# A transformer block on one core: a new instruction order, first-MLP partial sums split by token group, and a zero fill moved to the DMA queue

## The chip, the cores and the metric

The kernel runs on one core of a Trainium2 chip. A core has a matrix engine (PE, with its weight loads listed as PEld), a vector engine (DVE), a scalar engine (ACT), a general engine (POOL, also called GpSimd) and a sync engine (SP) which in this kernel issues nearly all the DMAs. Every engine works through its own list of instructions in order and waits on semaphores for the others. The metric is the device time of one execution in microseconds; the kernel before the change has a median of 255.73 us over three runs (255.32 to 256.43).

## The reference

One block on 2048 tokens of 512 features. A conditioning vector gives six modulation vectors (shift, scale and gate for each half). The first half is a layer norm, a modulation, and attention with 32 heads of 16 features in which a token sees itself and the 255 tokens before it. The second half is a layer norm, a modulation, another layer norm, and an MLP that mixes *tokens*: it contracts over the 2048 tokens, not over the features.

```python
h = _layernorm(x) * (1 + ca) + sa
x = x + ga * attention(h, wqkv, wo)       # 32 heads, window 256
h = _layernorm(x) * (1 + cb) + sb
# _B_ref(h):
    h = _layernorm(x)
    u = einsum('bsd,sf->bdf', h, w1) + b1   # contract over 2048 tokens, F = 1792
    u = gelu(u)
    y = einsum('bdf,fs->bds', u, w2) + b2   # contract over F
x = x + gb * y.transpose
```

## The kernel before

The tokens are cut into 16 tiles of 128 (`sc` 0 to 15), the tiles into four groups of 512 tokens (`G` 0 to 3). For each group the kernel normalizes and transposes its tokens (`proj`), projects them to queries, keys and values (tiles `QT`, `KT`, `VT`), runs attention, and closes the group with `post`: output projection (`pa`), residual (`x`), the two layer norms, and `hb`, the normalized input of the MLP, one tile for each 128 tokens.

Attention is 75 *chunks*. A chunk is one set of score matmuls on PE (`pss`, `psb`, called S in the code), two exponentials on ACT (`et<-pss`, `et<-psb`), a mask on DVE (`et<-et,maskt`), and, when a unit of chunks is complete, the value and sum matmuls on PE (`po`, called AV), a logarithm and exponential on ACT (`lz`), and a product on DVE (`OT`). Seven `et` buffers lie between the exponentials and the value matmuls.

The first MLP matmul (`pu`) needs, for each of 14 blocks of 128 columns of `w1` (`fc` 0 to 13), the sum over the 16 token tiles: 224 matmuls of 128x512. Its first half, tiles 0 to 7, is done during attention as *partial sums*: eight matmuls for each `fc`, then a copy from PSUM to a float32 tile `part[fc]` (`partials`, L1039). The second half, tiles 8 to 15, comes mostly after attention; `tail` (L1247) adds the partial sum (`a`), applies the GELU (`g`) and the gate (`guT`). Then the second MLP matmul `py` (238 matmuls) runs from `w2r` and `guT`, and each of its 16 output tiles is added to the residual and stored.

The weights `w1` come in 14 loads of 512 KB, one for each pair of `fc` and half of the tokens (`load_w1`, L1026); the second half takes the buffer of the first, and so its load waits until the partial sums have read that. `w2` comes in 14 loads of 512 KB (`e_w2`, L1231) into memory that attention held, so they start when attention is over. All of these, and the small copies `vs` and the transposes of `proj`, are issued by SP, in the order of its list.

The order of all instructions is not left to a scheduler. Every piece of work is an `Op` with possible engines, an estimated cost and what it depends on; `ORDER` (L60) is a fixed list of the operations, found offline with those costs, and `CHOSEN` (L114) names the engine where an operation can run on more than one. `run_schedule` (L154) emits them in that order; the costs in the code now matter only for the choice of PSUM slots. `e_w2` is one operation with cost 0.0, the fourteen loads in it included.

Of the kernel before, what the change touches and what calls it, by code (L numbers as in the profile page):

```python
# [9 lines left out]
ACT = mybir.ActivationFunctionType  # L10
# [3 lines left out]
P = 128  # L14
# [12 lines left out]
PART_A = 3  # L27
PART_AT = 20.0
# [3 lines left out]
X_READY = [3.0, 3.75, 11.7, 12.0]  # L32
MOD_READY = [4.7, 6.7, 6.9, 7.4]
W_READY = [8.35, 9.25, 9.25, 11.0, 14.0]
# [17 lines left out]
ZSCALE = 2.0 ** -32  # L52

# [59 lines left out]
]  # L113
CHOSEN = {  # L114
    "ACT": [
        48, 50, 72, 74, 95, 1017, 1034, 1039,
    ],
    "DVE": [
# [4 lines left out]
    ],  # L123
    "POOL": [
        712, 714,
    ],
}
BATCH = True
XT_AFTER = -0.7
W1_AFTER = 2.0  # L130
AV_POS = 0.2
LZ_POS = 0.0
# [4 lines left out]
class Op:  # L137
# [5 lines left out]
    def __init__(self, name, eng, cost, emit, deps=(), pos=0.0, cls=None, alloc=None, ready=0.0, extra=0.0, behind=()):  # L143
# [5 lines left out]
        self.done = None  # L149
        Op.count += 1  # L150
        self.n = Op.count

# [1201 lines left out]
```

## Time and profile before

| what | value |
|---|---|
| median of 3 runs | 255.73 us (255.32 to 256.43) |
| time of the profiled execution | 258.61 us |
| its span, first to last instruction | 256.8 us |
| mean granted clock of PE | 0.993 |
| busy: PE / DVE / ACT / POOL | 241.1 / 200.6 / 179.9 / 133.0 us |
| exponentials, 75 of 128x1536 and 75 of 128x512 | 110.8 and 46.9 us of ACT |
| `pu` matmuls, 224 | 52.6 us |
| `py` matmuls, 238 | 48.7 us |
| DMA | 27.02 MB, mean 105 GB/s |

The span is what the profile's page and its views show; the profiled execution's own time is 1.8 us longer than the span, and 2.9 us longer than the median of the runs. "Busy" of PE is the modelled time in the array: matmuls are pipelined, so a busy PE need not be at its peak. A wait is put down to what ended it last.

### The profile page before, as it was taken

The numbers are of one execution on the slowest core, as the hardware profiler recorded it, in microseconds if no ns is written. First come the engines' busy times: TensorE is split into PE (matmuls) and PEld (weight loads), VectorE is DVE, ScalarE is ACT, GpSimd is POOL, SyncE is SP. The second block draws the span as 40 slices with busy tenths as digits, with TensorE's granted clock in tenths as the row PEclk, the third lists the DMA queues.
The fourth block names the chain that finished last, engine by engine and source line by source line (L and its number), as shares of the span: only waits on it lengthen the run. The fifth ranks groups of instructions, "written<-read, shape, count | busy, mean of one in ns | idle before, by whom it ended". The sixth has DMA issues, their size and how long they took to land.

```text
span 256.8 us, 8133 instructions
## 1 busy us (share of the span) xinstructions
PE 241.1 (94%) x3427; PEld 122.2 (48%) x3427; DVE 200.6 (78%) x392; ACT 179.9 (70%) x255; POOL 133.0 (52%) x237
## 2 busy tenths in 40 slices
PE   7988989899998999979999999999999999999994
PEld 2665635444443454434545454446444444444443
DVE  4589999998899999998658879799869864444442
ACT  4399999999999999998999999998138510000000
POOL 8288977999999897896914389190000000000000
PEclk9999999999999999989999999999999999999999
DMA  7998360246254400060030003351899601111111
GB/s 222 326 349 252 12 80 3 42 114 159 61 120 60 116 3 3 9 182 0 5 92 14 3 3 84 106 142 37 326 332 387 232 22 41 58 48 41 41 43 41
DMA packets 41341, 27.02 MB, mean 105 GB/s; under 512 B 11992, under 2 KB 37208, under 8 KB 41304
## 3 DMA queue, kind: packets, MB, share of 16 engines
q1 hardware_dynamic: 41008, 25.97, 36.2%
q8 instruction: 27, 0.44, 0.7%
q10 hardware_dynamic: 296, 0.53, 0.6%
q14 instruction: 10, 0.08, 0.1%
HBM read 22.03 MB, written 2.10 MB: 94 GB/s over the span
## 4 chain that ended last, share of the span: by engine, by line
PE 61%; POOL 12%; DVE 10%; ACT 8%; issue 4%; DMA 3%; SPq 0%; DVEq 0%; POOLq 0%
PE pu L234 20%; PE py L234 19%; PE po L234 7%; ACT et L234 6%; PE pss L234 6%; POOL VT L234 4%; PE pa L234 3%; DVE et L234 3%; POOL xn L234 3%; POOL KT L234 2%; PE pk L234 2%; DMA w1p<-in_B_w_dram 2%; PE pv L234 2%; ACT lz L234 1%; DVE vb L234 1%
## 5 line engine op out<-in xcount | busy, mean ns | idle before, releaser
L234 ACT ACTIVATE et<-pss 128x1536 bf16<-128x1536 f32 x75 | 110.8, 1477 | 3.3 <-PE psb L234 1.7
L234 PE MATMUL pu<-hb,w1p 128*128 128x512 bf16 x224 | 52.6, 380 | 0.0
L234 DVE TENSOR_TENSOR et<-et,maskt 128x1024 bf16<-128x1024 bf16 (+2 forms) x79 | 48.5, 628 | 2.7 <-ACT et L234 2.6
L234 PE MATMUL py<-guT,w2r 128*128 128x512 bf16 (+1 forms) x238 | 48.7, 366 | 0.5 <-DVE otile L234 0.5
L234 ACT ACTIVATE et<-psb 128x512 bf16<-128x512 f32 x75 | 46.9, 626 | 0.0
L234 PE MATMUL pss<-QT,KT 32*128 32x64 bf16 (+3 forms) x720 | 30.0, 232 | 6.6 <-ACT et L234 5.0
L234 PEld LDWEIGHTS <-w2r 128*128 128x128 bf16 x238 | 23.3, 98 | 26.0 <-issue 0.7
L234 PE MATMUL po<-et,VT 128*32 128x64 bf16 (+3 forms) x960 | 32.3, 237 | 1.0 <-DVE kb L234 0.6
L234 PEld LDWEIGHTS <-w1p 128*128 128x128 bf16 x224 | 20.4, 98 | 25.0 <-issue 2.5
L234 PE MATMUL po<-et,ones_bd 128*32 128x256 bf16 (+3 forms) x624 | 32.0, 271 | 0.0
L234 POOL TENSOR_SCALAR KT<-kb,mask_par 128x512 bf16<-128x512 bf16 (+1 forms) x38 | 27.4, 732 | 7.2 <-ACT kb L234 5.8
L234 DVE TENSOR_TENSOR otile<-py,xr 128x512 bf16<-128x512 f32 (+1 forms) x17 | 11.2, 660 | 25.3 <-PE py L234 25.2
L234 PEld LDWEIGHTS <-KT 32*128 32x128 bf16 x960 | 15.8, 93 | 31.1 <-issue 28.9
L234 PE MATMUL psb<-QT,KT 32*128 32x64 bf16 (+3 forms) x240 | 29.5, 232 | 0.0
L234 PEld LDWEIGHTS <-VT 128*32 128x32 bf16 x960 | 19.6, 97 | 12.9 <-issue 10.7
L234 POOL TENSOR_SCALAR xn<-x,rs,nm 128x512 bf16<-128x512 bf16 x24 | 22.8, 951 | 1.4 <-DVE h L234 0.5
L234 DVE BATCH_NORM_STATS2 st<-x 128x6 f32<-128x512 bf16 x32 | 21.4, 682 | 2.2 <-DMA x<-in_A_x_dram 2.1
L234 PE MATMUL pk<-h1T,wqkv 128*128 128x256 bf16 (+2 forms) x108 | 21.3, 326 | 0.6 <-DVE vb L234 0.5
L234 PEld LDWEIGHTS <-wqkv 128*128 128x128 bf16 x164 | 13.8, 99 | 13.4 <-issue 6.0
L234 DVE TENSOR_TENSOR OT<-po,lz 128x256 bf16<-128x256 f32 x32 | 13.3, 416 | 8.2 <-ACT lz L234 8.2
L234 PE MATMUL pv<-wqkv,h1T 128*64 128x256 bf16 (+1 forms) x112 | 17.2, 321 | 0.4 <-DVE OT L234 0.4
L234 PE MATMUL pa<-wod,OT 128*128 128x512 bf16 x64 | 17.0, 380 | 0.4 <-DVE kb L234 0.2
(99 smaller groups left out, 324.1 us busy)
## 6 DMA issues: line engine op xcount, KB each, us to landing
w1p<-in_B_w_dram SPq DMA_DIRECT2D x14, 512.0 KB, 5.0
w2r<-in_B_w_dram SPq DMA_DIRECT2D x14, 512.0 KB, 7.8
x<-in_A_x_dram SPq DMA_DIRECT2D x16, 128.0 KB, 5.2
wmod<-in_w_mod_dram SPq DMA_DIRECT2D x4, 512.0 KB, 8.6
out_dram<-otile SPq DMA_DIRECT2D x15, 128.0 KB, 1.7
wqkv<-in_A_wqkv_dram SPq DMA_DIRECT2D x4, 256.0 KB, 4.9
vs<-vb SPq DMA_DIRECT2D x24, 32.0 KB, 3.0
wmod<-in_w_mod_dram ACTq DMA_DIRECT2D x2, 256.0 KB, 3.7
```

The lines of the kernel that those rows point to most:

```text
L234: ins = call(*args, **kwargs)
```

## The change

Five things are changed.

1. **Order and engines.** `ORDER` and `CHOSEN` are new lists, and the estimated costs are new (POOL's are lower: `xn` 0.77 instead of 0.88). More operations may run on DVE instead of POOL: the normalization `xn`, the key split `kk`, and the copies into `VT`. The operations that were classed "D" (dense 128x128 matmuls) are classed "AV" like the value matmuls, so that the estimate charges no change between the two kinds.
2. **Partial sums by token group.** For `fc` 0 to 9 (`EARLY = 10`) the partial sum is made in two parts of four matmuls: tiles 0 to 3 first, copied to `part[fc]`, and later tiles 4 to 7, which DVE adds to `part[fc]`. For `fc` 10 to 13 it stays eight matmuls. `w1` is loaded in 28 quarters of 256 KB (tokens by group of four tiles). Quarters 0 and 2, and 1 for the early pairs, share one buffer for each pair (`w1s`); the others have their own (`w1r`).
3. **Zero fill.** The buffer `VT[2]` was cleared by four memsets on POOL; it is now cleared by two DMAs of 512 KB that SP issues, from a zero tile `nothing`, which also replaces the zero tile `warm`.
4. **Start.** 12 warm-up matmuls instead of 16: ten at the beginning, two after the transpose of the conditioning vector, and none between the modulation matmuls and the first key matmuls.
5. A helper `mm` stands for `te.matmul`; with `NEAR_RUN = 0` its tiled branch is never taken.

```diff
-NPART = 14
-PART_A = 3
-PART_AT = 20.0
+EARLY = 10
+EARLY_AT = 6.0
+EARLY_STEP = 1.4
...
+NEAR_RUN = 0
...
+    def mm(dst, lhsT, rhs, start, stop):
+        if not Op.quad:
+            te.matmul(dst, lhsT=lhsT, rhs=rhs, start=start, stop=stop, skip_group_check=True)
+            return
...
-    warms = [op("warm", "PE", 0.86 if i < 4 else 0.43, lambda e, i=i: e_warm(e, 2, i == 0), pos=-7, cls="D", ready=1.4 if i < 4 else 4.8)
-             for i in range(8)]
+    warms = [op("warm", "PE", 0.86, lambda e: e_warm(e, 2), pos=-7, cls="D", ready=1.4) for i in range(6)]
...
-    def dense(name, pieces, emit, deps, pos, cls="D", alloc=None, ready=0.0):
+    def dense(name, pieces, emit, deps, pos, cls="AV", alloc=None, ready=0.0):
...
-            xn_ops.append(op("xn", "POOL", 0.88, lambda e, i=i: e_xn(e, i), deps=[st] + xn_ops[-1:] + transposed[G - 1][i : i + 1],
+            xn_ops.append(op("xn", {"POOL": 0.77, "DVE": 0.35}, 0.77, lambda e, i=i: e_xn(e, i), deps=[st] + xn_ops[-1:] + transposed[G - 1][i : i + 1],
...
-        zeros[2] = [
-            op("z", "POOL", 0.93, lambda e, n=n: po.memset(VT[2][:, 2 * n : 2 * n + 2, :, :], 0.0), deps=k_done[0, 1][-1:], pos=1.0 + n)
-            for n in range(4)
-        ]
+        zeros[2] = []
+        for n in range(2):
+            zeros[2].append(op("z2", "SP", 2.6, lambda e, n=n: dma.dma_start(
+                out=VT[2][:, 4 * n : 4 * n + 4, :, :].rearrange("p b a d -> p b (a d)"),
+                in_=nothing[:].unsqueeze(1).to_broadcast([P, 4, D]),
+            ), deps=zeros[2] + k_done[0, 1][-1:], pos=14.0 + n, ready=30.0, extra=1.0))
...
+    def load_w1(pair, quarter):
+        first = quarter in (0, 2) or (quarter == 1 and pair < EARLY // 2)
+        name = f"w1{'s' if first else 'r'}{pair}"
+        t = box["w1" if first else "B"].tile([P, 4, 2 * P], BF, name=name, tag=name)
+        dma.dma_start(out=t[:], in_=w1_v[:, 4 * quarter : 4 * quarter + 4, 2 * P * pair : 2 * P * (pair + 1)])
+        w1t[pair, quarter] = t
...
+            def e_pe(e):
+                if first:
+                    part[fc] = box["A" if fc < EARLY else "B"].tile([P, D], F32, name=f"part{fc}")
+                    copy(e, part[fc][:], box["p", fc][:])
+                else:
+                    ve.tensor_tensor(out=part[fc][:], in0=box["p", fc][:], in1=part[fc][:], op=ALU.add)
...
+        early = {}
+        for fc in range(EARLY):
+            pos = start_of(2) + EARLY_AT + fc * EARLY_STEP
+            early[fc] = group(fc, 0, [loads[fc // 2, 0], *done[:4]], pos, True)
+            if fc % 2:
+                load(fc // 2, 1, [early[fc - 1], early[fc]], pos + 0.5)
...
+            if fc % 2:
+                second[fc // 2] = [
+                    load(fc // 2, 2, part_ops[-2:], pos + 0.5),
+                    load(fc // 2, 3, [released] + (part_ops[-2:] if fc >= EARLY else []), max(pos, start_of(NG) - 10.0) + 0.6),
+                ]
```

Built, the two kernels stand against each other as follows. PE does the same matmuls but for four warm-ups fewer. DVE has 420 instructions instead of 394, POOL 222 instead of 242, ACT 260 in both. SP's list of DMAs ends, before the change, with five `w2r` loads, the last two loads of `w1` (512 KB each), nine `w2r` loads and the output; after the change with fourteen `w2r` loads, the last two loads of `w1` (256 KB each: `w1s` of pair 6 and of pair 4, tiles 8 to 11) and the output.

More of the change, by code (lines that the diff above doesn't have):

```diff
@@ L149, in __init__ @@
         self.done = None
+        self.tiled = False
         Op.count += 1
@@ L159, in run_schedule @@
     assert len(ORDER) == len(ops)
+    runs = []
+    for o in (ops[i] for i in ORDER if "PE" in ops[i].engs):
+        if not runs or runs[-1][0].cls != o.cls:
+            runs.append([])
+        runs[-1].append(o)
+    for run in runs:
+        sums = [n for n, o in enumerate(run) if o.name == "AV"]
+        if run[0].cls == "AV" and sums:
+            for a, b in zip([-1] + sums, sums + [len(run)]):
+                if b - a <= NEAR_RUN:
+                    for o in run[a + 1 : b]:
+                        o.tiled = True
     for i in ORDER:
@@ L310 @@
     modw = tc.alloc_tile_pool(name="modw", bufs=1, side="right")
-    warm = modw.tile([P, D], BF, name="warm")
-    nc.vector.memset(warm[:], 0.0)
+    warm = nothing
     wmod = modw.tile([P, ND, 6 * D], BF, name="wmod")
@@ L387, in copy @@
             ve.tensor_copy(out=out, in_=in_)
+    def mm(dst, lhsT, rhs, start, stop):
+        if not Op.quad:
+            te.matmul(dst, lhsT=lhsT, rhs=rhs, start=start, stop=stop, skip_group_check=True)
+            return
+        for j in range(4):
+            rows = slice(32 * j, 32 * j + 32)
+            te.matmul(
+                dst[rows], lhsT=lhsT[:, rows], rhs=rhs, start=start, stop=stop, tile_position=(0, 32 * j), skip_group_check=True,
+            )
     def bank(shape, dtype, name):
@@ L672, in e_hh @@
                         e_h(e, 2 * i + 1)
-                    hs[half].append(op("h1T", {"ACT": 0.94, "DVE": 0.7}, 0.9, e_hh, deps=[z, o_fm], pos=base + 1.5))
+                    hs[half].append(op("h1P", {"ACT": 0.94, "DVE": 0.7}, 0.9, e_hh, deps=[z, o_fm], pos=base + 1.5))
                     a.frees = hs[half][-1:]
@@ L730, in e_mm @@
                     w0 = (1 - n) * D + g8 * P
-                    te.matmul(
-                        box["kq", g8][:, n, :], lhsT=wqkv[:, dc, w0 : w0 + P], rhs=h1T[:, dc, cols],
-                        start=(dc == 0), stop=(dc == ND - 1), skip_group_check=True,
+                    mm(
+                        box["kq", g8][:, n, :], wqkv[:, dc, w0 : w0 + P], h1T[:, dc, cols],
+                        (dc == 0), (dc == ND - 1),
                     )
@@ L857, in e_h @@
                     )
-            h_ops.append(op("h1T", {"POOL": 2.05, "DVE": 0.7}, 0.9, e_h, deps=xt_ops + [o_fm], pos=p_tr))
+            h_ops.append(op("h1T", {"POOL": 1.75, "DVE": 0.66}, 0.9, e_h, deps=xt_ops + [o_fm], pos=p_tr))
         mms = []
@@ L866, in e_q @@
                 for dc in (2 * n, 2 * n + 1):
-                    te.matmul(
-                        box["q", g8][:], lhsT=wqkv[:, dc, g8 * P : (g8 + 1) * P], rhs=h1T[:, dc, :],
-                        start=(dc == 0), stop=(dc == ND - 1),
+                    mm(
+                        box["q", g8][:], wqkv[:, dc, g8 * P : (g8 + 1) * P], h1T[:, dc, :],
+                        (dc == 0), (dc == ND - 1),
                     )
@@ L886, in e_k @@
                 for dc in (2 * n, 2 * n + 1):
-                    te.matmul(
-                        box["k", g8][:], lhsT=wqkv[:, dc, D + g8 * P : D + (g8 + 1) * P], rhs=h1T[:, dc, :],
-                        start=(dc == 0), stop=(dc == ND - 1),
+                    mm(
+                        box["k", g8][:], wqkv[:, dc, D + g8 * P : D + (g8 + 1) * P], h1T[:, dc, :],
+                        (dc == 0), (dc == ND - 1),
                     )
@@ L924, in e_v @@
                 for dc in (2 * n, 2 * n + 1):
-                    te.matmul(
-                        box["v", tb][:], lhsT=h1T[:, dc, tb * P : (tb + 1) * P], rhs=wqkv[:, dc, 2 * D : 3 * D],
-                        start=(dc == 0), stop=(dc == ND - 1),
+                    mm(
+                        box["v", tb][:], h1T[:, dc, tb * P : (tb + 1) * P], wqkv[:, dc, 2 * D : 3 * D],
+                        (dc == 0), (dc == ND - 1),
                     )
@@ L1040, in partials, with load, e_rel @@
         opened = op("w1", "SP", 0.0, e_w1, deps=mod_ops + [o_fm, masks_built], pos=start_of(1) + 2.0, extra=-2.0)
-        loaded = []
+        loads = {}
+        chain = []
+        def load(pair, quarter, deps, pos):
+            name = f"w1{'abcd'[quarter]}"
+            o = loads[pair, quarter] = op(name, "SP", 1.3, lambda e: load_w1(pair, quarter), deps=deps, pos=pos, extra=W1_AFTER)
+            return o
+        def e_rel(e):
+            wpool.release()
+            box["B"] = ctx.enter_context(tc.tile_pool(name="partB", bufs=1, side="right"))
@@ L1051, in e_p, with group @@
+        def group(fc, lo, deps, pos, first):
+            hi = 8 if first and fc >= EARLY or not first else 4
+            def e_p(n):
                 if n == 0:
                     box["p", fc] = bank([P, D], F32, "pu")
-                for sc in (2 * n, 2 * n + 1):
-                    te.matmul(
-                        box["p", fc][:], lhsT=w1s(sc, fc), rhs=hb[sc][:], start=(sc == 0), stop=(sc == 7),
-                    )
-            def e_pe(e, fc=fc):
-                if fc == PART_A:
-                    wpool.release()
-                    box["B"] = ctx.enter_context(tc.tile_pool(name="partB", bufs=1, side="right"))
-                    for pair in range(NPART // 2, NF // 2):
-                        load_w1(pair, 1)
-                part[fc] = box["A" if fc < PART_A else "B"].tile([P, D], F32, name=f"part{fc}")
-                copy(e, part[fc][:], box["p", fc][:])
@@ L1067, in partials @@
-            behind = [proj_last[NG - 1]] if fc >= PART_A else []
-            a, z = dense("p", [0.431] * 4, e_p, [loaded[fc // 2]] + done + behind, pos, alloc="od")
-            g = op("pe", {"ACT": 0.5, "DVE": 0.6}, 0.6, e_pe, deps=[z] + part_ops[-1:], pos=pos)
-            a.frees = [g]
-            part_ops.append(g)
-            if fc % 2 == 1:
-                second[fc // 2] = op("w1h", "SP", 1.35, lambda e, fc=fc: load_w1(fc // 2, 1), deps=[g], pos=pos + 0.5, extra=W1_AFTER)
+                for sc in (lo + 2 * n, lo + 2 * n + 1):
+                    mm(
+                        box["p", fc][:], w1s(sc, fc), hb[sc][:], (sc == lo), (sc == hi - 1),
+                    )
@@ new lines, in e_pe @@
+            def e_pe(e):
[4 more added lines that the diff above has]
+                    ve.tensor_tensor(out=part[fc][:], in0=box["p", fc][:], in1=part[fc][:], op=ALU.add)
+            a, z = dense("p", [0.431] * ((hi - lo) // 2), e_p, deps, pos, alloc="od")
+            g = op("pe" if first else "pd", {"ACT": 0.5, "DVE": 0.6} if first else "DVE", 0.68, e_pe,
+                   deps=[z] + ([released] if fc >= EARLY else []) + ([] if first else [early[fc]]), pos=pos)
@@ new lines, in group @@
+            a.frees = [g]
+            return g
+        early = {}
[4 more added lines that the diff above has]
+                load(fc // 2, 1, [early[fc - 1], early[fc]], pos + 0.5)
+        for pair in range(EARLY // 2, NF // 2):
+            load(pair, 1, [released], start_of(NG) - 11.0 + pair - EARLY // 2)
+        for fc in range(NF):
+            at = start_of(3)
+            pos = at + fc * (start_of(NG) - PART_END - at) / NF
+            if fc < EARLY:
+                g = group(fc, 4, [loads[fc // 2, 1], *done[4:]], pos, False)
+            else:
+                g = group(fc, 0, [loads[fc // 2, 0], loads[fc // 2, 1], *done], pos, True)
+            part_ops.append(g)
+            if fc % 2:
[3 more added lines that the diff above has]
+                ]
```

78 lines of the change are left out of this document (36 added, 42 removed), and 119 rows, old and new, of tables (CHOSEN, ORDER).

## The prediction

> **What bounds the kernel now.** I read the page's 40 slices first, then the chain of work that ended last, then windows, the timelines of the engines, and SP's own timeline.
>
> The slices, each 6.4 us:
>
> ```profile
> PE   7988989899998999979999999999999999999994
> DVE  4589999998899999998658879799869864444442
> ACT  4399999999999999998999999998138510000000
> ```
>
> ACT is full from slice 2 to slice 27, some 20 to 175 us; only PE is full to the end. So there are two stages: attention, paced by ACT's exponentials with PE and DVE hardly less full, and a tail of about 79 us in which PE alone counts.
>
> Windows of 10 us (PE, PEld, DVE, ACT, POOL busy with the number of instructions, PE's granted clock, DMA share, GB/s):
>
> ```profile
> 110.00:120.00 10.00, 7.75 (x171) 4.29 (x170) 9.18 (x19) 8.73 (x12) 7.90 (x15) 0.83 0.42 115
> ...
> 150.00:160.00 10.00, 10.00 (x194) 5.01 (x193) 8.74 (x15) 9.77 (x15) 9.00 (x11) 1.00 0.17 41
> ```
>
> Over the sixteen windows from 20 to 180 us ACT is busy 155.6 of 160 us: a better order can win 4.4 us there and no more. The largest piece, 1.3 us, is in 110 to 120, the only window of attention in which PE's clock is down. PE's timeline there (start, us, matmuls):
>
> ```profile
> 113.22 0.29 PE L234 MATMUL pss<-QT,KT 32*128 32x128 bf16 x3 [1.72 <-ACT et L234]
> ...
> 115.17 1.68 PE L234 MATMUL pk<-h1T,wqkv 128*128 128x512 bf16 x4
> ```
>
> PE had waited 1.72 us, and then four matmuls that take 1.04 us elsewhere took 1.68: half speed until 116.8, where the next scores start, 3.5 us after the wait.
>
> The end of the chain (start, us, what):
>
> ```profile
> 177.84 1.83 PE pu L234 x8
> 179.67 0.86 PE pa L234 x4
> 180.53 0.43 PE pu L234 x2
> 180.96 0.86 PE pa L234 x4
> 181.83 22.88 PE pu L234 x106
> 204.71 46.87 PE py L234 x224
> ```
>
> From 177.84, where the last value matmuls end, PE runs without a gap, 22.88/106 = 0.216 us for each dense matmul. I call this moment T. In the same moment SP can start to load `w2`, into the memory that attention leaves:
>
> ```profile
> 177.93 2.90 SPq L234 DMA_DIRECT2D w2r<-in_B_w_dram  x5
> 184.88 0.99 SPq L234 DMA_DIRECT2D w1p<-in_B_w_dram  x2
> 185.92 8.25 SPq L234 DMA_DIRECT2D w2r<-in_B_w_dram  x9
> ```
>
> The last two loads of `w1` go after five of the fourteen `w2` loads. Windows of 2 us show how long the sixteen loads take:
>
> ```profile
> 184.00:186.00 2.00, 2.00 (x11) 0.90 (x10) 1.56 (x6) 0.86 (x3) 0.00 (x0) 1.00 1.05 409
> ...
> 200.00:202.00 2.00, 2.00 (x11) 0.93 (x10) 2.00 (x5) 1.44 (x2) 0.00 (x0) 1.00 1.05 389
> 202.00:204.00 2.00, 2.00 (x11) 0.93 (x10) 1.44 (x5) 0.98 (x2) 0.00 (x0) 1.00 0.45 169
> 204.00:206.00 2.00, 2.00 (x11) 0.88 (x9) 1.75 (x5) 1.21 (x3) 0.00 (x0) 1.00 0.00 0
> ```
>
> The DMA share is at 1 and the rate at 290 to 409 GB/s; the thirteen windows from 178 to 204 add up to 8.4 MB, which is 16 loads of 0.524 MB. The last ends near 202.9, T+25.0. And the view of the tile `w2r` says what a load in a full queue waits:
>
> ```profile
> DMA to landing us min/median/max: 3.3/7.8/11.0
> ```
>
> **The tail: the step that decides.** In the built order of the changed kernel SP issues all fourteen `w2r` loads first, and the last two `w1` loads (pair 6, then pair 4; 0.262 MB each) behind them. All are on one queue. Bytes ahead of and in the last: 14 x 0.524 + 2 x 0.262 = 7.86 MB, 0.52 MB less than before, 1.4 us at 385 GB/s: T+23.6, and I add 0.6 us for its completion (between 0 and the 1.7 us that the page gives an output store from issue to landing): T+24.2. The bounds are T+21.2 (389 GB/s all the way after a first 1 us) and T+28.5 (about 290 GB/s, the slower loaded windows).
>
> PE's list after T is: 6 `pu`, 8 `pa`, then 106 `pu`, then `py`. Pair 4's weights for tiles 8 to 11 are first read by the 55th of the 106. So PE wants them at T + (6 + 8) x 0.216 + 0.1 + 54 x 0.216 = T+14.8. (The `hb` tiles that it needs before are no later than in the trace: the last were made at 189.19 to 189.93, T+11.3 to 12.1, and are first read by the 43rd, T+12.2.) PE takes its list in order, so everything behind waits: 52 `pu`, all of `py`, and through them `a`, `g`, `guT` and the stores. **Stall: 24.2 - 14.8 = 9.4 us** (6.4 to 13.7).
>
> After a stall of 9.4 us PE starts at half speed; by the row above that lasted 3.5 us, a loss of 1.7 us (0 if the clock stays, 3.4 if it takes two such stretches). Then 52 x 0.216 = 11.2 us of `pu`, and from the start of `py` to the end of the span 256.8 - 204.71 = 52.1 us as before. End: T + 24.2 + 11.2 + 1.7 + 52.1 = T+89.2, against 256.8 - 177.9 = T+78.9 now: **+10.3 us**.
>
> **Attention: when T comes.**
>
> *Start.* Now six warm-up matmuls stand between the modulation matmuls and the first keys: they run from 7.98 to 10.49, each 0.427 apart, at half speed, while the last input of the keys, `h1T` on DVE, is there at 9.36. Without them the keys start 1.1 us earlier. But full speed began at 10.7, in the middle of the keys; if that comes later too, 8 key and 4 query matmuls (0.056 and 0.109 us apart) cost 0.9 us more, and the next ones a little more. Between -1.1 and +0.5; I take **-0.6**, the middle of the two cases with and without speed. [...]
>
> *Class changes on PE.* Two dense matmuls at 147.08 are followed by `po` at 147.62: 0.54 for 2 x 0.216, so a change costs 0.11 us, between dense and value matmuls too, which the new order's costs take as free. Counted in the built orders, changes up to the tail rise from 194 to 223, and between chunks 49 and 73 from 56 to 72, where PE is as full as ACT: 16 x 0.11 = 1.8 us if PE paces that stage, 0 if ACT does. **+0.9**. The others, 13 x 0.11 = 1.4 us, lie in the earlier part, where PE waits for ACT; if that cover went, 1.4 more.
>
> *Early partial sums.* 40 `pu` (8.6 us) move from after chunk 51 to chunks 42 to 56. That does not shorten the tail: 124 `pu` follow the last scores, 122 before. It takes PE work out of the last stage and puts it where PE idles, so it can win only ACT's waits: the dip at 110 to 120 (1.2 us, if `pu` keep PE busy there; half: **-0.6**) and what is left of the 4.4 us (0 to 3.2; the later windows hold little of it: **-0.5**). The split costs ten additions on DVE instead of none, and 14 smaller `w1` loads of which none is new in bytes.
>
> *DVE and POOL.* DVE gains 10 additions (0.688, row of `a`), 1 `part` copy (0.686), 8 `xn` (0.41), 6 `hb` (0.40), 8 `VT` copies (not shown on DVE; between a 128x4 copy, 0.15, and a 128x256 cast, 0.41; 0.3), 6 key splits (0.34 to 0.43), 1 net evacuation of 256 columns (0.41), and loses 6 `h1T` (0.43), 3 pairs of `h` (1.02), 1 `vb` (0.68), 1 copy (0.43): 18.5 - 6.8 = +11.7 us. POOL loses 4 memsets (3.8), 8 `xn` (7.6), 6 `hb` (5.4), 8 `VT` copies (4.2), 6 key splits (4.5) and gains 6 `h1T` (at 0.95 of `xn`) and 3 pairs of `h` (2.9): -11 us. DVE's load falls on 100 to 175 us, where the windows leave it 11.4 us idle from 120 to 180; that idle time hides it, and I cost it **0**. With the cover half gone it is +4. POOL was on the chain only from 51 to 84 us, where ACT loses 0.6 us in all: its relief is in the term above. ACT trades evacuations: +0.2 us, nothing.
>
> *Zero fill.* Two DMAs of 0.5 MB on SP, 1.4 us each at 385 GB/s, between transposes and `vs` copies: they delay a `vs` by that at most; between 0 and 1.4, and POOL's 3.8 us lay beside ACT. 0.
>
> Sum for T: -0.6 + 0.9 - 0.6 - 0.5 = **-0.8 us** (-5.5 to +6.3).
>
> **Sum.** The span goes from 256.8 to 256.8 + 10.3 - 0.8 = 266.3, the profiled execution from 258.61 to 268.1. That one is 2.9 us above the median of the runs shown, so on the median: 255.73 + 9.5 = **265.2 us**.
>
> **The rivals.**
> 1. *No stall; faster.* The two small loads overtake the large ones, or come early enough. Then the tail is T+3.1+22.9+52.1 = T+78.1, and the time 255.73 - 0.8 - 0.8 = 254.1 us. Against it: 16 loads at a full DMA share, and landings of 3.3 us in an empty queue and 11.0 in a full one, eight loads of 1.4 us. For it: no row shows a small load behind nine large ones. It decides below 1.3 us of stall.
> 2. *Only 1 to 2 us of stall*, since loads run faster than any window shows: about 255.7.
> 3. *The stall, and all ACT waits gone.* T comes 5.5 us earlier: 265.2 + 0.8 - 5.5 = 260.5. For it: less POOL work, 8.6 us of PE work moved forward. Against it: DVE and PE class changes fill the same room.
> 4. *The stall, and DVE paces attention.* DVE was 95.6 of 100 us busy from 20 to 120 and has 11.7 us more; with 4 us uncovered and the class changes in full: 265.2 + 4 + 0.9 = 270.1.
>
> That the change does less than it says holds for one part: the tiled matmuls are never taken, at no cost.
>
> **How the numbers follow.** My forecast 0.62, rival 1 0.08, rival 2 0.04, rival 3 0.12, rival 4 0.14. The range 259.5 to 270.5 holds the forecast with its bounds and rivals 3 and 4, less a tenth for their edges. A measurement of this kernel can tell about 0.5%, 1.3 us: faster 0.08 (rival 1), same 0.04 (rival 2), slower 0.88.
>
> **What would show it.** Right: SP's timeline with fourteen `w2r` loads and then two `w1s`; a gap of 6 to 14 us on PE among the 106 `pu`, ended by a DMA of `w1s`, some 15 us after the last value matmuls; half speed behind it; T between 172 and 184. The early keys near 9.5 us, and a clock of 1.0 at 110 to 120, would show the smaller terms. Wrong: PE without a gap in the tail, or a stall that waits for `hb`.

## The result, and the profile after

The changed kernel takes 272.51 us (median of 4 runs, 272.04 to 273.43) beside 255.9 us for the kernel before (4 runs): ratio 1.065, interval 1.062 to 1.069. The profiled execution took 273.43 us with a span of 271.7. The forecast was 265.2 us: slower, as it said, but 7 us slower still and outside the range.

The slices of the changed kernel's page, 6.8 us each:

```profile
PE   7789789999877899999999979999607999999992
DVE  4699999999999998899979999989700864543451
ACT  3699999999998899999999989950610530000000
PEclk9999999999999999999999999999966999999998
```

PE is no longer full to the end: it has a hole from about 195 to 205 us (the 0 and its neighbours), and the granted clock falls to 6 there. ACT is no longer full through attention: it is at 8 in two slices from 82 to 95 us and in one near 160 us, and DVE is at 9 in these. The end of the chain of waits of the changed kernel (start, us, what):

```profile
177.86 2.34 PE po L256 x104
...
185.27 10.11 DMA w2r<-in_B_w_dram
195.40 9.81 DMA w1s<-in_B_w_dram
205.26 9.00 PE pu L256 x33
214.26 0.05 issue
214.31 4.05 PE pu L256 x18
218.36 6.69 PE py L256 x31
```

The last value matmul ends at 180.18 (T). Then PE is not on the chain for 25 us; loads are. SP's timeline and PE's timeline of the changed kernel show the same from both sides:

```profile
180.27 12.80 SPq L256 DMA_DIRECT2D w2r<-in_B_w_dram  x14
194.05 3.42 SPq L256 DMA_DIRECT2D w1s<-in_B_w_dram  x2
```

```profile
190.93 4.05 PE L256 MATMUL pu<-hb,w1r 128*128 128x512 bf16 x17
205.26 1.89 PE L256 MATMUL pu<-hb,w1s 128*128 128x512 bf16 x4 [10.28 <-DMA w1s<-in_B_w_dram]
```

The four matmuls behind the 10.28 us gap take 1.89 us, against 1.04 elsewhere. Windows of 4 us in this stretch (PE, PEld, DVE, ACT, POOL busy, granted clock, DMA share, GB/s):

```profile
194.00:198.00 4.00, 0.98 (x5) 0.25 (x3) 3.64 (x8) 2.92 (x5) 0.00 (x0) 1.00 1.05 387
198.00:202.00 4.00, 0.00 (x0) 0.00 (x0) 0.00 (x0) 0.73 (x2) 0.00 (x0) 0.56 1.05 380
202.00:206.00 4.00, 0.74 (x2) 0.28 (x3) 0.00 (x0) 0.00 (x0) 0.00 (x0) 0.50 0.48 129
206.00:210.00 4.00, 4.00 (x14) 1.55 (x13) 0.00 (x0) 0.00 (x0) 0.00 (x0) 0.66 0.01 4
```

While nothing but the loads runs the DMA share is at 1 (1.05 in the rows, 380 to 387 GB/s); the clock drops during the gap, to 0.50, is 0.81 from 208 to 210 us and 1.00 from 210 to 220. So the stall is what the forecast described. What it did not foresee lies ahead of it, in windows of 10 us of attention:

```profile
80.00:90.00 10.00, 7.46 (x176) 4.34 (x172) 9.94 (x21) 9.18 (x14) 6.42 (x16) 1.00 0.36 79
90.00:100.00 10.00, 8.67 (x139) 3.88 (x140) 9.97 (x19) 8.95 (x13) 7.83 (x10) 1.00 0.02 5
...
160.00:170.00 10.00, 9.54 (x152) 3.91 (x156) 9.76 (x18) 8.33 (x12) 5.28 (x10) 1.00 0.01 3
```

DVE is busy 9.8 to 9.97 of 10 us in them, ACT only 8.3 to 9.2.

Where the time went is seen best by chunk. The table takes, for each chunk, the start of its 128x1536 exponential on ACT, and compares the lengths of the stretches in three profiles: the one of the kernel before that the forecast was made from, a later profile of the same kernel with a span of 254.8 (e14_before_third, below; just over half of the 77 runs of that kernel that were made beside the experiments have 254.0 to 254.9), and the changed kernel.

| stretch | before, 256.8 us | before, 254.8 us | after | after less the second |
|---|---|---|---|---|
| start to chunk 1 | 12.89 | 10.94 | 10.67 | -0.27 |
| chunk 1 to 33 | 69.26 | 69.31 | 69.97 | +0.66 |
| chunk 33 to 45 | 25.30 | 25.31 | 28.03 | +2.72 |
| chunk 45 to 49 | 9.78 | 9.64 | 7.99 | -1.65 |
| chunk 49 to 65 | 34.21 | 34.21 | 35.05 | +0.84 |
| chunk 65 to 69 | 8.50 | 8.51 | 9.96 | +1.45 |
| chunk 69 to T | 17.90 | 17.89 | 18.51 | +0.62 |
| T to the start of the last product `otile` | 75.96 | 75.97 | 87.28 | +11.31 |
| from there to the end of the span | 3.0 | 3.0 | 4.2 | +1.2 |

The last line is a matter of the single execution: with the same code it is 3.0 us in the profiles of e1_w1_first and e2_pe_kept_busy. So is most of the line of chunk 1 to 33: with the same code up to there, it is 69.22 us in e1 and 69.14 in e2, and 69.2 to 70.2 in the other variants of the changed kernel.

### The profile page after: what moved, and what is told of

Its sections match the earlier page's. It is cut to its first block, busy times and chain, and to the rows that moved or that the text cites. A ratio compares the mean times of both kernels' runs of the same rounds, so it can differ in the third digit from the quotient of the medians.

```text
span 271.7 us, 8105 instructions
## 1 busy us (share of the span) xinstructions
PE 237.2 (87%) x3379; PEld 118.9 (44%) x3423; DVE 211.3 (78%) x418; ACT 181.4 (67%) x255; POOL 119.6 (44%) x217
## 4 chain that ended last, share of the span: by engine, by line
PE 45%; DVE 17%; ACT 12%; DMA 7%; issue 4%; SPq 2%; ACTq 0%
PE py L256 18%; ACT et L256 11%; PE pu L256 10%; PE po L256 6%; DVE et L256 5%; PE pss L256 4%; DMA w2r<-in_B_w_dram 4%; DMA w1s<-in_B_w_dram 4%; PE pa L256 3%; DVE st L256 2%; DVE h L256 2%; SPq L256 2%; ACT lz L256 2%; DVE OT L256 1%; PE pq L256 1%
## 5 line engine op out<-in xcount | busy, mean ns | idle before, releaser
L256 ACT ACTIVATE et<-pss 128x1536 bf16<-128x1536 f32 x75 | 109.6, 1461 | 5.3 <-PE psb L256 3.1
L256 PE MATMUL pu<-hb,w1s 128*128 128x512 bf16 x141 | 39.6, 391 | 12.3 <-DMA w1s<-in_B_w_dram 10.3
L256 DVE TENSOR_TENSOR et<-et,maskt 128x1024 bf16<-128x1024 bf16 (+2 forms) x79 | 46.7, 608 | 1.3 <-ACT et L256 1.1
L256 ACT ACTIVATE et<-psb 128x512 bf16<-128x512 f32 x75 | 45.6, 609 | 0.0
L256 POOL TENSOR_SCALAR KT<-kb,mask_par 128x512 bf16<-128x512 bf16 (+1 forms) x32 | 23.6, 747 | 12.9 <-DVE kb L256 12.5
L256 PEld LDWEIGHTS <-VT 128*32 128x32 bf16 x960 | 17.7, 96 | 21.0 <-issue 19.7
L256 PEld LDWEIGHTS <-w1s 128*128 128x128 bf16 x152 | 13.3, 100 | 29.3 <-DMA w1s<-in_B_w_dram 10.8
L256 ACT ACTIVATE g<-a,b1FM 128x512 bf16<-128x512 f32 x14 | 9.8, 720 | 17.7 <-DVE guT L256 13.5
L256 DVE TENSOR_TENSOR a<-pu,part 128x512 f32<-128x512 f32 x14 | 9.3, 685 | 14.5 <-PE pu L256 14.5
L256 PE MATMUL pu<-hb,w1r 128*128 128x512 bf16 x69 | 18.0, 387 | 0.2 <-issue 0.2
```

The source lines that it names most:

```text
L256: ins = call(*args, **kwargs)
```

## The experiments

### The stall

*e1_w1_first.* In the changed kernel's `ORDER` the two late loads (1060 and 1036) go ahead of `w2` (1062).

```diff
-    ... 915, 719, 934, 1062, 1060, 930, 935,
-    937, 931, 936, 938, 1036, 1092, ...
+    ... 915, 719, 1060, 1036, 934, 1062, 930, 935,
+    937, 931, 936, 938, 1092, ...
```

> The changed kernel with its last two w1 loads (pair 6, pair 4) issued ahead of the fourteen w2r loads; nothing else moves. Theory (the step of the tail): the 10.28 us gap goes and with it the half-speed stretch behind it, 1.7 to 1.9 us, so 272.5 - 12.1 = 260.4 us (259.5 to 261.5), with PE free of gaps from the last value matmul to the first py, and the end 78 to 80 us after the last value matmul. Rival (PE would wait at that place for something else, hb or the rate of all loads): a gap of several us stays and the time stays above 265 us. In neither case does it come under the kernel before's 255.7: attention ends 2.3 us later than there, and the exit took 1.4 us longer.

260.19 us (259.10 to 261.25), ratio 1.014 (1.009 to 1.019). The chain of e1 from the last value matmuls on:

```profile
179.09 2.31 PE po L256 x104
181.41 1.42 PE pu L256 x6
182.83 1.73 PE pa L256 x8
184.56 22.88 PE pu L256 x106
207.43 46.87 PE py L256 x224
```

The 106 `pu` take 22.88 us without a gap, as in the kernel before. The two loads' place in SP's list cost 272.5 - 260.2 = 12.3 us of the 16.6 that the change cost. The rest, some 4 us, comes before T.

*e2_pe_kept_busy.* The stall stays, but PE works through it.

```diff
+                    if sc == lo and fc // 2 == 4 and "filled" not in box:
+                        box["filled"] = True
+                        for _ in range(45):
+                            te.matmul(ftiles[fc][:], lhsT=nothing[:, 0:P], rhs=nothing[:], start=True, stop=True)
```

> The changed kernel with 45 extra matmuls of zeros, 45 x 0.216 = 9.7 us, put on PE directly before its first read of the late w1 quarter, so that PE works through the stall instead of standing; the load comes no earlier. Theory (the clock drops after a stall and half speed costs 1.7 to 1.9 us): the gap on PE shrinks to about 0.5 us, the pu behind it keep 0.216 us each, and the time falls to 272.5 - 1.8 = 270.7 us (270.3 to 271.2). Rival (the slow matmuls behind the stall are slow for another reason, the two loads' traffic for example, or there is no clock cost): no change, 272.0 to 273.0.

270.08 us (268.72 to 270.84), just under the expected range. PE's timeline of e2:

```profile
194.77 9.88 PE L256 MATMUL pu<-nothing 128*128 128x512 bf16 x45
204.98 1.04 PE L256 MATMUL pu<-hb,w1s 128*128 128x512 bf16 x4 [0.34 <-DMA w1s<-in_B_w_dram]
```

The four real matmuls now take 1.04 us, and the granted clock is 1.00 from 190 to 220 us. From T to the first `py` it is 36.10 us instead of 38.02: 1.92 us of the cost was the clock, the other 10 the wait itself.

*e3_before_w1_last.* The mirror: in the kernel before, loads 1040 and 1029 go behind `w2` (1041).

```diff
-    ... 1072, 1052, 1040, 949, ... 950, 1029, 1087, ... 952, 1079, 1041, 1059, ...
+    ... 1072, 1052, 949, ... 950, 1087, ... 952, 1079, 1041, 1040, 1029, 1059, ...
```

> The kernel before with its last two w1 loads (512 KB each, pair 6 then pair 5) issued behind the fourteen w2r loads instead of among them. Theory: sixteen loads land by T+25.0 as they do now, PE wants pair 5 at its 79th matmul after T, T + 78 x 0.216 + 0.1 = T+17.0, so it stands for 8.0 us and then loses 1.7 to 1.9 us at half speed: 255.8 + 9.8 = 265.6 us (264 to 267). Rival (the order of loads in one queue does not matter, or the changed kernel's stall comes from its quarters): no gap, 255 to 256.5 us.

268.19 us (267.14 to 270.36), ratio 1.043 (1.037 to 1.048): above the expected 264 to 267. PE's timeline of e3:

```profile
204.05 12.51 PE L234 MATMUL pu<-hb,w1p 128*128 128x512 bf16 x46 [9.76 <-DMA w1p<-in_B_w_dram]
```

The stall is there, 9.76 us instead of 8.0, since the last load landed at T+26.7, not T+25.0; 46 matmuls at 0.216 would take 9.9 us and took 12.5, so half speed (a granted clock of 0.50 from 202 to 206 us and 0.63 from 206 to 210) cost 2.6. (T+25.0 is where the traffic ends in the kernel before. Its own last load, issued at 193.4 us, landed 10.9 us later, at 204.29: T+26.4.) The order of loads alone makes this stall, in either kernel.

### Attention: DVE, and POOL beside it

The timeline of DVE in the changed kernel at the second thin place of ACT, and POOL's at the same time:

```profile
156.20 1.26 DVE L256 TENSOR_TENSOR h<-h,bc_sb 128x512 bf16<-128x512 bf16 x1
157.39 1.37 DVE L256 TENSOR_TENSOR et<-et,maskt 128x512 bf16<-128x512 bf16 x1
158.68 1.27 DVE L256 TENSOR_TENSOR part<-pu,part 128x512 f32<-128x512 f32 x2
...
161.68 1.49 DVE L256 TENSOR_TENSOR et<-et,maskt 128x1024 bf16<-128x1024 bf16 x1
```

```profile
155.92 1.27 POOL L256 TENSOR_TENSOR h<-xn,bc_cb 128x512 bf16<-128x512 bf16 x1 [0.94 <-DVE xn L256]
157.26 1.21 POOL L256 TENSOR_TENSOR h<-h,bc_sb 128x512 bf16<-128x512 bf16 x1
158.47 1.68 POOL L256 TENSOR_SCALAR xn<-x,rs,nm 128x512 bf16<-128x512 bf16 x2
...
161.47 1.15 POOL L256 TENSOR_TENSOR h<-h,bc_sb 128x512 bf16<-128x512 bf16 x1
```

DVE's `h`, mostly 0.39 to 0.50 elsewhere, takes 1.26; a mask product of 128x512, mostly 0.41, takes 1.37; one of 128x1024, mostly 0.68, takes 1.49. Each began 0.1 to 0.3 us after an instruction of POOL had begun, and ended 0.3 to 0.6 us after that instruction's end. The two additions `part` at 158.68, one of whose inputs lies in PSUM, took 1.27 us for both beside POOL's `xn`, no more than the 0.69 each of other places, and the one at 160.48 took 0.69 beside POOL's `h` of 160.23. What decides which instruction of DVE is lengthened, these rows do not show; what POOL's `h` costs is tested by e5 below.

The kernel before has this too, in the same stretch, chunk 65 to 69, beside POOL's `h` of 153.94 and 155.22 us:

```profile
154.05 1.64 DVE L234 TENSOR_TENSOR et<-et,maskt 128x1024 bf16<-128x1024 bf16 x1
155.94 1.04 DVE L234 TENSOR_TENSOR et<-et,maskt 128x512 bf16<-128x512 bf16 x1
```

Over that stretch DVE's instructions are longer than usual by 2.0 us in all before and 2.1 after (an estimate: each duration less the median of its kind in the two traces). So DVE's long instructions there are not what the change added. What it added is work for DVE. Windows of chunk 33 to 45 and of chunk 65 to 69 (columns as above), the kernel before first, then the changed kernel:

```profile
82.15:107.46 25.31, 23.88 (x445) 11.93 (x445) 24.60 (x45) 25.12 (x35) 21.79 (x40) 1.00 0.14 34
151.44:159.94 8.50, 8.50 (x173) 4.37 (x167) 8.33 (x15) 8.27 (x12) 7.67 (x8) 1.00 0.19 46
```

```profile
80.64:108.66 28.02, 23.66 (x461) 12.09 (x469) 27.12 (x53) 26.06 (x35) 19.61 (x37) 1.00 0.14 31
151.71:161.67 9.96, 8.37 (x122) 3.48 (x124) 9.51 (x15) 8.60 (x12) 8.35 (x11) 1.00 0.38 107
```

DVE was nearly full there already, and is busy 2.5 and 1.2 us longer, in stretches that are 2.7 and 1.5 us longer.

*e5_h_on_dve*, built on e1: the five `h` that `CHOSEN` has on POOL (250, 476, 480, 706, 710) leave that list, and so run on DVE.

```diff
-        71, 76, ... 249, 250, 258, ... 473, 476, 477, 480, 486, ... 703, 706, 707, 709, 710, 716, ...
+        71, 76, ... 249, 258, ... 473, 477, 486, ... 703, 707, 709, 716, ...
```

> e1_w1_first with the five products h = xn * bc_cb + bc_sb that run on POOL put on DVE (two instructions of 0.41 us each there, some 2.6 us on POOL). Beside them single DVE instructions in the trace take 1.26 and 1.37 us in place of 0.42 and 0.41. Theory (DVE is held up by POOL while both run such instructions): those DVE instructions fall to 0.4 to 0.5 us, which pays for the 0.85 us of work each that DVE takes over; the steps from chunk 33 to 37 and from 65 to 69 are each shorter by 0.5 to 1.5 us, in all 260.2 - 1.5 = 258.7 us (257.5 to 259.7). Rival (DVE only has too much work): 5 x 0.85 us more on DVE make these steps longer by 0.5 to 1.5 us, 261 us or more.

258.57 us (258.09 to 260.08, 10 runs), ratio 1.008 (1.004 to 1.012). The same place on DVE in e5:

```profile
155.06 0.41 DVE L256 TENSOR_TENSOR h<-xn,bc_cb 128x512 bf16<-128x512 bf16 x1
155.50 0.42 DVE L256 TENSOR_TENSOR h<-h,bc_sb 128x512 bf16<-128x512 bf16 x1
155.85 0.42 DVE L256 TENSOR_TENSOR et<-et,maskt 128x512 bf16<-128x512 bf16 x1
156.18 0.42 DVE L256 TENSOR_TENSOR h<-xn,bc_cb 128x512 bf16<-128x512 bf16 x1
```

DVE has more instructions, and is done sooner: chunk 33 to 37 took 9.44 us instead of 10.16, chunk 65 to 69 9.25 instead of 9.97.

*e4_no_part_adds*, built on e1: of the second partial sums only one column is copied, and none is added.

```diff
-                    ve.tensor_tensor(out=part[fc][:], in0=box["p", fc][:], in1=part[fc][:], op=ALU.add)
+                    ve.tensor_copy(out=part[fc][:, 0:1], in_=box["p", fc][:, 0:1])
```

> e1_w1_first without the ten additions of the second partial sum on DVE (each a copy of one column instead; left out: the sums of tiles 4 to 7 for ten fc, so the output is not the reference's). In after and e1 alike the exponentials from chunk 65 to chunk 69 take 1.46 us longer than in the kernel before, and 0.8 us are lost in small steps from chunk 49 to 65. Theory (DVE paces attention at 120 to 166 us because of 10 x 0.69 us more work): the step from chunk 49 to chunk 69 is 1.5 to 2.3 us shorter than in e1. Rival (PE paces it: 16 more class changes and the pu that were moved forward): under 0.5 us shorter.

Chunk 65 to 69 took 9.20 us instead of 9.97, but chunk 49 to 65 35.04, as in e1: 0.8 us in all, not 1.5 to 2.3. The time of the one run was 258.71 us. (Chunk 37 to 41 was 0.56 shorter too, where nothing had been edited; so single stretches there scatter by that much.) DVE paces 65 to 69 and not 49 to 65.

*e8_h_and_adds*: both edits together.

> e5_h_on_dve and e4_no_part_adds together (built on e1_w1_first; the additions of the second partial sum left out). Theory (the 1.46 us that the step from chunk 65 to 69 takes longer than in the kernel before are DVE's: half the additions, half the time POOL holds it up): the two add up, the step is 1.3 to 1.6 us shorter than the 9.97 us of e1 and so as long as in the kernel before (8.50). Rival (either alone already reaches what another engine allows): 0.7 to 0.9 us shorter, as each alone.

Chunk 65 to 69 took 8.59 us, as long as in the kernel before (8.50). So DVE is what costs the 1.45 us, and it is relieved by half by either edit. The additions are the half that the change put there; the time that DVE's instructions lose beside POOL's was there before (2.0 us there and 2.1 after, by the estimate above), and whether the other half comes from the rest of DVE's new work or from the new order is open. The time, 261.03, was one run with a late start (first keys at 9.62 us).

*e6_less_dve*, built on e1: four pieces go from DVE to POOL.

```diff
     "DVE": [
-        ... 256, 257, ... 523, ... 534, ...
     "POOL": [
+        256, 257, 523, 534,
```

> e1_w1_first with four pieces of work between 86 and 97 us (two hb, one pair of copies into VT from vs and one from vb) on POOL instead of DVE, 1.9 to 2.7 us of DVE time; POOL stands idle for 2.8 us at 83 and 1.8 us at 93. Theory (DVE's load sets the pace at 80 to 100): the steps from chunk 33 to chunk 45 are 1.0 to 2.3 us shorter than in e1, 260.2 - 1.5 = 258.7 us (257.8 to 259.6). Rival (POOL's side is as full, its instructions hold DVE up, or PE sets the pace): within 0.5 us of e1.

Chunk 33 to 45 took 26.72 us instead of 28.02, as the theory said. But chunk 45 to 49 then took 9.45 instead of 8.00, and the time, expected at 258.7, was 261.18 us (259.95 to 262.39): nothing won.

*e11_h_and_less*: e5 and e6 together.

> e5_h_on_dve and e6_less_dve together (both on e1_w1_first). From chunk 33 to 45 the kernel before takes 25.30 us, e1 28.02, e5 27.11, e6 26.72. Theory (all of this loss is DVE's own load and POOL holding it up, each about half): the two gains add up, the step is 25.6 to 26.2 us, and the time 258.6 - 1.2 = 257.4 us if PE's clock holds at 110 us, 258.6 if it falls there as in e6. Rival (another engine sets this stretch once DVE is relieved of either): 26.5 us or more, and the time 258.3 us or more.

259.16 us (258.86 to 260.94), more than expected. Chunk 33 to 45: 26.02 us, so 2.0 of the 2.7 us lost there are shown to be DVE's (give or take the 0.56 of scatter). Chunk 45 to 49 took 9.64 us, and DVE's timeline of e11 says why:

```profile
106.78 0.43 DVE L257 TENSOR_TENSOR h<-xn,bc_cb 128x512 bf16<-128x512 bf16 x1 [1.85 <-POOL xn L257]
107.25 0.42 DVE L257 TENSOR_TENSOR h<-h,bc_sb 128x512 bf16<-128x512 bf16 x1
107.59 0.41 DVE L257 TENSOR_SCALAR xn<-x,rs,nm 128x512 bf16<-128x512 bf16 x1
107.91 0.69 DVE L257 COPY part<-pu 128x512 f32<-128x512 f32 x1
```

DVE now stands for 1.85 us behind POOL's `xn`, and the copy `part` behind it, which gives back a PSUM bank, comes that much later; PE waits 1.54 us for it. In a fixed order a stretch that gets faster runs into the next wait of that order.

*e7_fewer_pu*, built on e1: 40 matmuls of the split partial sums left out.

```diff
+                    if fc < EARLY and lo < sc < hi - 1:
+                        continue
```

> e1_w1_first with the inner two of the four matmuls left out in each of the twenty partial sums of fc 0 to 9 (40 of 224 pu, 8.6 us of PE; the output is not the reference's). From chunk 49 to 65 the changed kernel loses 0.83 us against the kernel before in steps of 0.15 to 0.25, which neither the additions nor the h products touched. Theory (there PE paces, with more class changes and the pu that were moved forward): the step from chunk 49 to 65 is 0.6 to 1.2 us shorter than the 35.04 us of e1. Rival (DVE or ACT): under 0.2 us shorter. The step from 65 to 69, where DVE is the theory, should lose under 0.3 of its 9.97 us.

Chunk 49 to 65 took 34.16 us instead of 35.04 (0.88 shorter), so PE paces that stretch. But chunk 65 to 69 took 10.76 instead of 9.97, against what was expected. DVE has the same instructions there, and is busy for 10.4 of the 10.76 us, so what PE saved ahead of it was lost again; why the stretch is longer than in e1 is open. The time of the one run was 259.61 us.

### The start and the clock

*e0_before_again*, *e14_before_third* and *e15_before_fourth* are the kernel before, unchanged, in three more profiles.

> The kernel before, unchanged, profiled a second time. Its profiled execution in the prediction had a span of 256.8 us while most others had 253.3 to 255.1. Theory (a): the difference lies in the warm-up and in the clock dip at 110 to 120 us, so that in this run the first keys start before 10.0 us or the dip costs under 1 us, and the steps between the chunks elsewhere are the same within 0.1 us. Theory (b): it lies in the exit, last product to end of span 3.0 us there and elsewhere 1 to 2 us less.

> The kernel before, unchanged, profiled a third time; both profiles so far (spans 256.8 and 256.9) were of its rarer, longer kind, while most runs have 254.0 to 254.9. Theory: a run of the common kind has the full clock before 5 us, the six warm-ups ahead of the keys at 0.216 us each, keys at 8.2 to 9.3 us, the same dip at 110 to 120 us, and its last value matmul at 175.3 to 175.7 us, with 79.0 us from there to the end as in the first profile. Rival: the start is the same and the 2.4 us lie behind the last value matmul. A span of 256.5 or more tells nothing new.

> As e14_before_third, a fourth profile of the kernel before: the same theory and rival, in case the third falls into the longer kind again.

Spans 256.9, 254.8 and 257.4 us. The first and third are like the forecast's profile (keys at 10.31 and 10.68). e14 is a common run. PE's timeline at the start, the forecast's profile first, then e14:

```profile
5.63 1.01 PE L234 MATMUL pss<-warm 128*128 128x512 bf16 x2
...
7.98 2.72 PE L234 MATMUL pss<-warm 128*128 128x512 bf16 x6
10.49 0.49 PE L234 MATMUL pss<-h1T,wqkv 128*128 128x128 bf16 x4
```

```profile
5.44 1.01 PE L234 MATMUL pss<-warm 128*128 128x512 bf16 x2
...
7.35 1.46 PE L234 MATMUL pss<-warm 128*128 128x512 bf16 x6
8.64 0.39 PE L234 MATMUL pss<-h1T,wqkv 128*128 128x128 bf16 x4
```

In e14 the six warm-ups run at full speed, and the keys come 1.85 us earlier; that is carried through to T (175.81 against 177.84), and 79.0 us follow in both. So the theory of e14 holds for the six, the keys, the dip and the 79.0 us; T came 0.1 us later than its range. It does not hold in one point: the full clock did not come before 5 us, since the two warm-ups at 5.44 still take 1.01. In e0 and e15 these two took 0.59, at full speed, and the six behind them were at half speed again (mean granted clock of the span 0.987 and 0.986, against 0.993 in e14). The theory of e0 holds only for the start: the dip was in all four profiles.

*e6_before_start*: the kernel before, in its own order, with the changed kernel's warm-ups.

```diff
-    lambda e, i=i: e_warm(e, 2, i == 0)
+    lambda e, i=i: e_warm(e, (2, 3, 3, 2, 0, 0, 0, 2)[i], i == 0)
```

> The kernel before with the start of the changed one alone: ten warm-up matmuls at the beginning, two after the transpose, none between the modulation matmuls and the first keys. Theory (the start carries through, since ACT paces attention): full speed by 4 us, keys at 8.3 instead of 10.5, first exponential 1.5 to 2.2 us earlier, and 1.0 to 2.0 us of it reach the end: 253.8 to 254.8 us, ratio 0.992 to 0.996. Rival (the gain is eaten in the first chunks, or the clock does not come earlier): within 0.3% of the kernel before, 255.0 to 256.5 us.

257.53 us (12 runs), ratio 1.005 (1.002 to 1.008): no gain, and rather a loss of half a per cent. Its profile has keys at 9.07 and T at 176.71, earlier than the forecast's profile and later than e14's.

*e9_before_filled* and *e10_start_filled*: six matmuls in the wait of PE ahead of chunk 48, in the kernel before and in e6_before_start.

```diff
+                box["sb", i] = ps_b.tile([P, D], F32, name="psb")
+                if i == 47:
+                    for _ in range(6):
+                        te.matmul(box["sb", i][:], lhsT=identity[:], rhs=hb[0][:], start=True, stop=True)
                 box["sa"] = ps_a.tile([P, 3, D], F32, name="pss")
-                box["sb", i] = ps_b.tile([P, D], F32, name="psb")
```

> The kernel before with six extra matmuls of 128x512 (1.3 us) put ahead of the scores of chunk 48, in the 1.72 us in which PE waits there, into the buffer that these scores overwrite. Theory (that wait lets the clock fall, and half speed costs 1.2 us): where the kernel before has the dip, it is gone, the step from chunk 45 to 49 is 8.6 us instead of 9.78, and the median falls by 0.4 to 1.2 us, as often as the dip falls into a run: 255.0 to 255.8 us. Rival (the clock falls whatever PE does, or the six matmuls delay the scores): 255.8 to 257 us, and the step stays over 9.3 us.

> e9_before_filled with the start of the changed kernel as in e6_before_start. Theory (in e6 nearly every run had the dip, which is why its earlier start did not pay): without the dip 257.5 - 1.2 = 256.3 us, or 254.9 to 256.5; it would be the fastest of all if the start were worth what the two profiles showed. Rival (the start of the changed kernel is no gain in most runs): not faster than e9_before_filled.

In the profiles of both the dip is gone, chunk 45 to 49 takes 8.60 us, and 0.36 of what was won is given back by chunk 53. The median of e9 did not fall as expected. e9: 256.66 us, ratio 1.001 (0.998 to 1.004), with five spans of 253.5 to 254.1 and seven of 255.8 to 256.4; e10: 256.36 us, ratio 1.001 (0.999 to 1.004).

*e12_warm10* and *e13_warm12*: e9 with two and four more warm-ups at the beginning, the later eight kept.

> e9_before_filled (the kernel before without its clock dip) with ten warm-up matmuls instead of eight at the beginning, the other eight kept where the kernel before has them. Theory (the kernel before has two kinds of runs, spans about 253.5 and 255.8 without the dip, and the slow ones are those in which eight warm-ups did not bring the full clock and the next ones run at 0.427 us, as in its profile): with ten the clock comes in all runs, the six warm-ups ahead of the keys take 0.216 each, the keys start at 8.9 to 9.4 us, and nearly all spans are 253.3 to 254.3: median 255.3 us, ratio 0.995 to 0.998, faster than both kernels. Rival (the two kinds of runs have another cause, such as the loads or the exit): spans of 255.8 stay as frequent as in e9, 7 of 12, and the median stays at 256.0 to 257.

> As e12_warm10 with twelve warm-ups at the beginning. Theory: as e12, with the transpose of the conditioning vector up to 0.5 us later if the clock comes late: 255.3 to 255.8 us, no slow starts. Rival: as for e12.

e12: 256.02 us, ratio 0.998 (0.995 to 1.001), all twelve spans between 253.4 and 254.8; e13: 256.56 us, ratio 1.000 (0.997 to 1.003). The late starts are gone (6 of the 23 runs of the kernel before that were made beside these had 256.2 or more), so they were the clock's: the six took 2.72 us in the forecast's profile, whose record of the granted clock begins at 10.70 us, with 1.00, and 1.46 in e12's. But the medians did not fall to the 255.3 to 255.8 expected: the common run of the kernel before has keys at 8.64, e12 at 9.23, as the two added warm-ups ran at half speed ahead of the transpose (ten took 4.45 us, eight 3.59). No version tried is shown to be faster than the kernel before.

## Why the prediction was wrong, point by point

- **The tail** was right in place and mechanism: fourteen `w2r` loads, then two `w1s`; PE stops at the 55th of the 106 `pu`; half speed behind it; the rest as before. It cost 11.3 us instead of 10.3. The mis-sized term is the landing of the last load, T+25.0 instead of T+24.2. In it the 0.6 us for the completion is the part that failed: in the forecast's own profile the last load landed at T+26.4, 1.4 us after the traffic ended, and with the 1.4 us for fewer bytes taken off that gives T+25.0. The clock cost 1.7 us, as forecast (1.9 by e2); since it was 2.6 in e3, that it met the forecast so closely is in part luck.
- **T** is the step that failed: 0.8 us earlier was forecast, and it came 4.4 us later than in a common run of the kernel before. Within it, "that idle time hides it, and I cost it **0**", the term for DVE, is the error: 2.72 us at chunks 33 to 45 and 1.45 at 65 to 69, of which e11 and e8 give back 2.0 and 1.4. The forecast placed DVE's new load at 100 to 175 us, and read the cover off the windows from 120 to 180 us as one sum, but the work is not spread as the idle time is: in the changed kernel DVE is busy 9.8 of 10 us from 160 to 170, and from 80 to 100, where the kernel before had 0.3 us of 20 idle, it had no cover at all. DVE's instructions were also priced at their usual durations, and moving `h` to POOL counted as relief for DVE, though two of those beside POOL's `h` took 1.26 and 1.37 us, three times their usual time; e5, without five `h` on POOL, took 258.57 us against 260.19 in e1, so this costs time, but the kernel before lost as much to it at chunks 65 to 69, so the difference between the two does not lie there. Rival 4 had the mechanism, with 4 us at the same size as measured, and 0.14 of the chance; its time, 270.1, added it to a tail and a T that were each too early.
- **Class changes and moved `pu` on PE**, +0.9 forecast: +0.84 at chunks 49 to 65, where e7 shows that PE paces, and up to 0.62 more behind 69, which was not tested. The size is about right. Whether it is the class changes or the matmuls that the new order moved there, e7 does not tell apart.
- **The dip**, -0.6: the stretch that has it is 1.65 us shorter in the changed kernel, where the clock stays at 1.00. e9 shows that work for PE in that wait removes the dip, which brings 1.05 of this (8.60 instead of 9.64); the rest is the new order's. The dip is not in every run: the profiles with it have a mean granted clock of 0.986 or 0.993, those of e9, e10, e12 and e13 without it 0.998 to 1.000, and 27 of the 77 runs of the kernel before have 0.999 or 1.000. **Other waits of ACT**, -0.5: nothing was won; the +0.66 at chunks 1 to 33 is mostly a matter of the single execution.
- **The start**, -0.6: -0.27 against a common run. The forecast measured it against a profile whose own start was 1.95 us late, and took the 2.9 us between that profile and the median off as a constant. Against a run of that kind the change had more to win than in most runs. e6 shows that the new warm-ups win nothing in the median, and e10 with the dip removed neither. In nine profiles of the changed kernel and its variants the keys start anywhere from 8.23 to 9.62 us, and the traces show what goes with it. DVE's copy `sT`, which the modulation matmuls need, stands behind the second `st` and, in the new order, behind an `xn` too. Where DVE waits 0.70 to 1.28 us for the load of `x` ahead of that `st` (four profiles), the keys start at 9.10 to 9.62; in the five others at 8.23 to 8.50. No run changed that place, so this is not shown by a test.
- In all: 16.6 us measured, 9.5 forecast; of the 7.1 between them 5.2 are T, 1.0 the tail, and 0.9 the differences of single runs.

## What to carry to other kernels

When a list of transfers is reordered, look up for each of them when it is first read, and put those needed first ahead of the bulk: two loads of 256 KB behind 7 MB cost 12 us here. An engine with 5% idle time covers new work only where that work falls, so count its idle time window by window, and price an instruction beside what another engine does at that moment. Before a difference is taken off a profile, find out in which stretch that profile differs from the common run.

## What the runs showed of the hardware

- The VectorE instructions with two SBUF inputs shown above took 1.04 to 1.64 us instead of mostly 0.41 to 0.68 where GpSimd's `h` had started before them; additions with one input in PSUM took their usual 0.68 to 0.69 beside its `xn` and beside its `h`.
- The same wait of PE, 1.72 us, was followed by half speed in five of six profiles of the kernel before and its variants (a granted clock of 0.50 to 0.55 in the lowest window of 2 us), and in e3 by none; there the clock stayed at 1.00 from 108 to 120 us. Behind eight warm-up matmuls in a row (from 1.27 to between 4.58 and 4.87 us) the six ahead of the keys ran at full speed in one of four profiles of the kernel before (1.46 us for the six in e14, 2.72 in the forecast's profile); with ten, and the rest as it was, no late start was seen in twelve spans (e12). Why the same work met the full clock in one profile and not in another, no run shows.
- Two loads of 256 KB behind fourteen of 512 KB on one queue landed last, at 204.41 and 205.21 us, behind the last of the fourteen at 203.56: nothing overtook.
